# A fused delta-rule attention and two MoE layers: vector work re-queued behind later steps

## The chip, the cores and the metric

The kernel runs on one core of a Trainium2 chip. The metric is the time of one execution in device microseconds (us). Three runs of the kernel before gave 983.3, 986.69 and 988.2 us; their median is 986.69 us. The engines that matter here are TensorE (PE in the profile), VectorE (DVE), ScalarE (ACT), GpSimd (POOL, which here mostly issues DMAs) and SyncE (SP, which only issues DMAs). Each has its own queue of instructions and runs them in the order in which they stand there.

## The reference

Three things are computed one after the other. Shapes are 4 batches, 8 heads, 768 steps of 48 features, so that the attention's output is 3072 tokens of 384 features.

```python
# attention: a delta rule over 768 steps, for each batch and head
k_n = k / (norm(k) + 1e-06)
for t in range(S):
    y[t] = q[t] @ state
    state = state + beta[t] * outer(k_n[t], v[t] - state.T @ k_n[t])
x = y.transpose(0, 2, 1, 3).reshape(3072, 384)
# MoE 1, 384 -> 2048 -> 384
h = maximum(x @ w_in, 0.0); x = (h * h) @ w_out
# MoE 2, 384 -> 768 -> 384
h = maximum(maximum(x @ w1, x @ w2), x @ w3); out = h @ w_out2
```

## The kernel before, in words

The 768 steps are cut into 12 chunks of 64 (`NC`). A chunk of attention is computed in block form: inside a chunk, a triangular system of 64 by 64 per head is inverted in two halves of 32, and the halves are then merged.

**The solve** (`solve32`, `solve`, lines 280 to 288 and 678 to 695) inverts the 32 by 32 halves of two chunks at once on VectorE: a short preparation that begins with a copy of the diagonal (`ss`, L264), then 30 steps of two dependent instructions each (L285 and L287), then one multiplication (L288). The result goes to DRAM (`xt`, `finish32`) and comes back as `xb` and `x1` (`load_x`). There are six solves: chunks 0 and 1 in the prologue, 2 and 3 beside MoE(0) and MoE(1), then 4 and 5, 6 and 7, 8 and 9, 10 and 11 beside MoE(2), (4), (6) and (8). The solve also yields the norms of the keys, which TensorE transposes (`pt`, L277) and ScalarE copies to `normT` (L313).

**The attention of a chunk** (`attention(c)`, lines 383 to 537) is a generator of steps. `st0(p)` multiplies V by the norms (L436, "V's norm" below) and multiplies the keys and queries with the running state (`pA`, `pY`, L447), after which VectorE forms `r` (L450). `zz` transposes `x1` on VectorE (`xT`, L408) and makes `pZ` (L415) from `xb`; `ww` makes `pW` (L424) from `xT` and `z` and ScalarE copies it into `xb` (L431): this is the merge. `mm_u(p)` makes `pU` from `xb` and `r` (L457, copied to `u` at L462), `st2(p)` makes `pY` and the growth of the state `pD` (L497, L475; `Sb` added at L482; `yy` copied at L512), `st3(p)` transposes `yy` (`pT`, L518) and splits it into a high part `xh` (ScalarE, L521) and a low part `xl` (VectorE, L522). p is 0 or 1, two halves of the heads.

**MoE 1 of a chunk** (`moe_a(c)`, lines 540 to 586), called MoE(c) here, has 8 blocks s1 (18 matmuls of `p` from `xh` and `xl`, L552) and 8 blocks s2 (18 matmuls of `px`, L570), s2 two blocks behind s1. Between them ScalarE makes the high part `gh` (L558) and VectorE the low part `gl` (L559), which also frees the PSUM tile of s1 (there are two). The attention of chunk c+1 is interleaved with MoE(c), so that MoE(c+1) can start when `xh` and `xl` of chunk c+1 are there. Beside MoE(0), (1), (3), (5) and (7), `kkps` makes the Gram matrices of later chunks (`pk`, `pq`, L197; stored to DRAM as `kk` and `p`).

**What sets the order.** In the loop over chunks (lines 800 to 834) `steps` advances the main generator MoE(c) by 16 steps and after each one the others at given rates; `later(n, g)` lets n steps pass first and `part(g, n)` takes only n steps of a generator. A scheduler then orders the instructions of each engine by its own estimate of when they are ready. `behind(a, b)` forbids it to put a ahead of b on the same engine; it makes nobody wait for a semaphore. `last_gl[0]` is the newest `gl` and `last_vec[0]` the newest marked VectorE instruction (a transpose `xT` or a low part `xl`).

From MoE(9) on, `w3load` also loads and splits the words of `w1` and `w2`: four VectorE instructions for each piece (L110, L113, L114, L118) and two on ScalarE (L107, L115). Behind MoE(11) the second MoE runs alone (L857, L874).

Of the kernel before, what the change touches and what calls it, by code (L numbers as in the profile page):

```python
# [39 lines left out]
def delta_moe(ctx, tc, kc, ab, kt, vt, beta, beta32, beta16, kq, w_in, w_out, w1, w2, w3, w_out2, out):  # L40
# [32 lines left out]
    parted, last_gl, last_gh = [], [None], [None]  # L73
# [197 lines left out]
    def behind(ins, before):  # L271

        tc.add_manual_dep(ins, before.name, mybir.DependencyInfo(mybir.DependencyClass.NoSync, mybir.DependencyReason.DATA), reason="order")
# [6 lines left out]
    def solve(eng, M, n, u, a, tmp):  # L280

        for j in range(1, n - 1):
            m = n - 1 - j
            tv = tmp[0:u, 0:j * m].rearrange("p (a b) -> p a b", a=j)
            eng.tensor_tensor(out=tv, in0=M[:, 0:j, j].unsqueeze(2).broadcast_to([u, j, m]),  # L285
                              in1=M[:, j, j + 1:n].unsqueeze(1).broadcast_to([u, j, m]), op=ALU.mult)
            yield eng.tensor_tensor(out=M[:, 0:j, j + 1:n], in0=M[:, 0:j, j + 1:n], in1=tv, op=ALU.add)  # L287
        yield eng.tensor_tensor(out=M, in0=M, in1=a.unsqueeze(2).broadcast_to([u, n, n]), op=ALU.mult)  # L288
# [44 lines left out]
    def load_x(c):  # L333

        k21 = att.tile([128, B * Q, 32], F32, name="k21", tag="k21", bufs=1)
        x1 = att.tile([128, U2, 32], F32, name="x1", tag="x1", bufs=1)
        ds = []
        for t in range(2):
            if c:
                ds.append(pool.dma_start(k21[64 * t + 32:64 * t + 64], kk_d[c][32:64, t, :, 0:32]))  # L340
            for h in range(2):
                o, hs = 64 * t + 32 * h, slice(32 * h, 32 * h + 32)
                i = (pool if c else (nc.sync, act)[t]).dma_start(xb[o:o + 32, :, hs], xt_d[c][h, t].rearrange("u j i -> j u i"))
                if c:
                    ds.append(i)
                else:
                    x_loaded.append(i.ins)
        for t in range(2):
            for g in range(2):
                o = 64 * t + 32 * g  # L350
                i = (pool if c else (nc.sync, act)[t]).dma_start(x1[o:o + 32], xt_d[c][0, t, U2 * g:U2 * g + U2].rearrange("u j i -> j u i"))
                ds.append(i)
        for i in x_after:
            if c:
                for d in ds:
                    behind(d.ins, i)
        return k21, x1
# [21 lines left out]
    xh, xl, masked, last_act, last_vec = {}, {}, {}, [None], [None]  # L379
    second_out = []  # L380
    ops, normed, solved, solve_after, x_loaded = [], [], [], [], []

    def attention(c):
# [7 lines left out]
        def fresh(name, p, i, shape):  # L391
            if name == "r" and p and not c:
                t = pkp.tile(shape, F32, name="r1", tag="r1")
            else:
                t = att.tile(shape, F32, name=name, tag=name, bufs=1 if name == "r" else 2)
            tiles[c, p][i] = t
            return t
# [7 lines left out]
        def zz(k21, x1):  # L405
            xT = att.tile([128, U2, 32], F32, name="xT", tag="xT", bufs=1)
            z = k21[:, 0:U2]
            last_vec[0] = vec.transpose(out=xT, in_=x1).ins  # L408
            if c == 1:
                behind(last_vec[0], last_gl[0])  # L410
            pZ = ps_at.tile([128, U2, 32], F32, name="pZ", tag="at")
            for u in spread:
                for t in range(2):
                    lower = k21[last(t), u] if c else kss[u // U2][last(t), 0, u % U2, 0:32]
                    pe.matmul(pZ[part_(t, u), u % U2], lower, xb[last(t), u, 32:64], start=True, stop=True)  # L415
            last_act[0] = act.activation(out=z, in_=pZ, func=AF.Copy, scale=-1.0).ins
            merge.extend((xT, z))
# [15 lines left out]
        def st0(p):  # L433
            kq_, v = tiles[c, p][0:2]
            vn = v if c else fresh("r", p, 6, [128, U2, D])
            i = vec.tensor_mul(out=vn, in0=v, in1=normT[:, c, U2 * p:U2 * p + U2].unsqueeze(2).broadcast_to([128, U2, D]))  # L436
            if c < 2:
                behind(i.ins, last_gl[0] if c else solved[0])
            if not c:
                return  # L440
            pA = ps_at.tile([128, U2, D], F32, name="pA", tag="at")
            pY = ps_y.tile([128, U2, D], F32, name="pY", tag="y")
            tiles[c, p][8] = pY
            for u in range(U2):
                for i, ps in enumerate((pA, pY)):
                    for t in range(2):
                        pe.matmul(ps[half(t ^ i), u], kq_[feat(t), u, i], Sb[feat(t), U2 * p + u],  # L447
                                  start=not i or u == 0, stop=not i, skip_group_check=bool(i))
            r = fresh("r", p, 6, [128, U2, D])
            vec.tensor_sub(out=r, in0=v, in1=pA)  # L450
# [73 lines left out]
        k21, x1 = load_x(c)  # L524
# [1 line left out]
            load_att(c, 0)  # L526
        load_att(c, 1)
        if c:
            order = ((st0, 0),), ((zz, (k21, x1)),), *(((),) if c == 1 else ()), ((ww, 0),), ((mm_u, 0),), ((st2, 0),), ((st0, 1), (st3, 0)), ((mm_u, 1),), ((st2, 1),), ((st3, 1),)
        else:  # L530
            order = ((st0, 0), (st0, 1)), ((zz, (k21, x1)),), ((ww, 0),), ((mm_u, 0), (mm_u, 1)), ((st2, 0), (st2, 1)), ((st3, 0), (st3, 1)), ((state, 0), (state, 1))
        for fs in order:
# [117 lines left out]
    def part(g, n):  # L650
        for _ in range(n):
            next(g, None)
            yield
# [5 lines left out]
    if True:  # L659
# [18 lines left out]
        def solve32(g, load=(nc.sync, nc.sync), store=((nc.sync,) * 2,) * 2, landing=0):  # L678
            M, a, ready, norm = start32(g, load)
            for _ in range(landing):  # L680
                yield
            if landing:
                prep_after[:] = last_gl
            nm = ready()
            if not landing:
                normed.append(norm(nm))
            yield
            for n, i in enumerate(solve(vec, M, 32, 64 * len(HALVED[g]), a, tmp32)):
                for j in solve_after:
                    behind(i.ins, j)  # L690
                ops.append(i.ins)
                if landing and n == 12:
                    norm(nm)
                yield
            finish32(g, M, store)

        def later(n, g):
            for _ in range(n):
                yield
            yield from g  # L700
# [99 lines left out]
        for c in range(NC):  # L800
            extra = []
            if c + 1 < NC:
                extra.append((9 / 15.0, attention(c + 1)) if c > 1 else (13 / 15.0, later(3, attention(1))) if not c else (17 / 15.0, later(8, attention(2))))
            if c == 0:
                ws = weights()
                for _ in range(2):
                    next(ws)
                extra.insert(0, (1.0, ws))
            if c in KK:
                extra.append((1.0, kkps(HALVED[1], (at,), pool)) if c == 0 else (0.8, later(5, kkps(HALVED[2], (at,)))) if c == 1 else (0.6, kkps(HALVED[KK[c]], (at,))))  # L810
            if c in SOLVE:
                solve_next = solve32(SOLVE[c], landing=16 if c == 8 else 10) if c else solve32(1, (pool,) * 2)
                extra.append((5.0, later(45, part(solve_next, 20))) if c == 0 else (6.0 if c == 8 else 4.0, solve_next))
            if c == 1:
                extra.insert(0, (6.0, solve_next))
            if c == 1:
                kc_after.clear()
            if c == 1:
                solve_after[:] = last_vec
                prep_after.clear()  # L820
            if c == 2:
                solve_after.clear()
            if c == 9:
                after[:] = last_gl
                load_w3s = w3load((0, 1))
            if 9 <= c < NC - 1:
                extra.append((0.4, part(load_w3s, 6)))
            if c == NC - 1:
                pr.close()
                wb = ctx.enter_context(tc.tile_pool(name="wb", bufs=1, side="right", reuse_waits="tile"))  # L830
                first = []
                extra.append((0.6, chain(load_w3s, w3load((2,)))))
                extra.append((0.5, later(2, x2_steps(0, wb, first))))
            steps(moe_a(c, gp), *extra)
# [114 lines left out]
```

## Time and profile before

| what | value |
|---|---|
| median of three runs | 986.69 us |
| the profiled execution | 983.45 us |
| its span, first to last instruction | 981.7 us |
| mean granted clock of TensorE over the span | 0.956 of full speed |
| TensorE busy | 902.9 us (92%) |
| VectorE busy | 452.8 us (46%) |
| ScalarE busy | 414.3 us (42%) |
| GpSimd busy | 154.1 us (16%) |

The profiled execution takes 1.75 us more than its span, and is 3.24 us below the median. The page has TensorE busy in nine tenths or more of nearly every fortieth of the span from 147 us on; its waits lie ahead of that and at a few places behind. The views used below are the table by stretches (cut where the first matmul of each MoE(c) starts), the timeline of an engine with the idle time before each instruction, the groups of instructions by line with a mean duration, and the chain that ended last.

### The profile page before, as it was taken

Reading aid. Unit: us, or ns where it says so; the run is one execution under the profiler, and the core shown is the slowest. Engines: PE = TensorE matmul, PEld = TensorE weight load, DVE = VectorE, ACT = ScalarE, POOL = GpSimd, SP = SyncE. Lnnn points to the kernel's source line nnn. Section 1 sums busy time; section 2 is a strip of 40 time slices with the busy share of each in tenths; the row PEclk is TensorE's granted clock in tenths of the full one; section 3 lists DMA queues with packets and bytes.
Section 4 is the critical chain, followed back from the end, with each engine's and each line's share of the span. In section 5 each row is a group of like instructions: output and inputs, shape, how many; then the busy total and the mean of one; then the engine's idle time right before and its main releaser. Section 6 shows DMA issues by size and latency. Waiting matters only on the chain.

```text
span 981.7 us, 26638 instructions
## 1 busy us (share of the span) xinstructions
PE 902.9 (92%) x11674; PEld 830.0 (85%) x11674; DVE 452.8 (46%) x976; ACT 414.3 (42%) x817; POOL 154.1 (16%) x257
## 2 busy tenths in 40 slices
PE   5057879999999999999999899999999999999998
PEld 4057768989899999999999799999888888888887
DVE  2979577129422852394238344446621323232221
ACT  1946873345344544444444356565411212121111
POOL 3133310321312132114111320000100000000000
PEclk8567988989999999999999999999999999999999
DMA  9948721571554155415522532134400100000001
GB/s 206 320 111 254 224 83 50 138 193 54 147 142 128 54 147 154 116 54 147 157 75 65 141 113 85 49 101 135 137 9 25 41 24 25 17 17 17 17 17 41
DMA packets 77413, 98.84 MB, mean 101 GB/s; under 512 B 37312, under 2 KB 55024, under 8 KB 77296
## 3 DMA queue, kind: packets, MB, share of 16 engines
q1 hardware_dynamic: 55232, 54.29, 19.6%
q0 software_dynamic: 12992, 36.35, 12.8%
q10 hardware_dynamic: 9072, 6.49, 2.3%
q8 instruction: 92, 1.51, 0.6%
q14 instruction: 25, 0.20, 0.1%
HBM read 72.45 MB, written 24.64 MB: 99 GB/s over the span
## 4 chain that ended last, share of the span: by engine, by line
PE 69%; DVE 10%; DMA 8%; issue 6%; ACT 4%; POOL 2%; ACTq 0%; SPq 0%; DVEq 0%; POOLq 0%
PE p L857 23%; PE p L552 15%; PE px L570 14%; PE po L874 8%; DVE buf L287 3%; DVE buf L285 3%; PE pU L457 2%; DMA xb<-xt 2%; PE pY L497 2%; DMA v<-in_vt_dram 1%; DMA buf<-kk 1%; DMA xt<-buf 1%; PE pZ L415 1%; PE pk L197 1%; PE pW L424 1%
## 5 line engine op out<-in xcount | busy, mean ns | idle before, releaser
L570 PE MATMUL px<-gh,wout 128*128 128x256 f32 x1152 | 218.8, 289 | 1.2 <-issue 1.2
L857 PE MATMUL p<-x_h,w 128*128 128x512 f32 x648 | 203.5, 395 | 0.0
L570 PEld LDWEIGHTS px<-gh,wout 128*128 128x128 f32 x1152 | 180.9, 193 | 3.8 <-issue 1.1
L552 PE MATMUL p<-xh,win_h 128*128 128x256 f32 x576 | 169.6, 295 | 4.8 <-DVE gl L559 3.4
L552 PE MATMUL p<-xl,win_h 128*128 128x256 f32 x576 | 166.3, 292 | 3.7 <-DVE xl L522 3.7
L552 PE MATMUL p<-xh,win_l 128*128 128x256 f32 x576 | 165.8, 289 | 0.0
L570 PE MATMUL px<-gl,wout 128*128 128x256 f32 x576 | 164.3, 285 | 0.0
L857 PEld LDWEIGHTS p<-x_h,w 128*128 128x128 f32 x648 | 121.7, 188 | 27.0
L559 DVE TENSOR_TENSOR gl<-p,gh 128x512 fp32r<-128x512 f32 x96 | 65.9, 687 | 154.0 <-ACT gh L558 153.6
L857 PE MATMUL p<-x_l,w 128*128 128x512 f32 x324 | 128.1, 395 | 0.0
L552 PEld LDWEIGHTS p<-xh,win_h 128*128 128x128 f32 x576 | 113.0, 196 | 8.3 <-DVE gl L559 4.2
L556 ACT ACTIVATE p<-p 128x512 f32<-128x512 f32 x96 | 56.1, 584 | 149.3 <-PE p L552 145.6
L552 PEld LDWEIGHTS p<-xl,win_h 128*128 128x128 f32 x576 | 112.5, 197 | 4.9 <-DVE xl L522 3.9
L552 PEld LDWEIGHTS p<-xh,win_l 128*128 128x128 f32 x576 | 113.2, 196 | 0.3
L570 PEld LDWEIGHTS px<-gl,wout 128*128 128x128 f32 x576 | 111.1, 193 | 0.3
L863 DVE TENSOR_TENSOR mx<-p,mx 128x512 f32<-128x512 f32 x36 | 24.9, 691 | 128.6 <-PE p L857 128.6
L865 ACT CAST hh<-mx 128x512 fp32r<-128x512 f32 x36 | 22.3, 621 | 127.6 <-DVE mx L864 127.6
L857 PEld LDWEIGHTS p<-x_l,w 128*128 128x128 f32 x324 | 61.0, 188 | 14.5
L287 DVE TENSOR_TENSOR buf<-buf 128x30 f32<-128x30 f32 (+9 forms) x180 | 59.5, 331 | 5.4
L285 DVE TENSOR_TENSOR buf<-buf 128x30 f32<-128x30 f32 (+9 forms) x180 | 59.2, 329 | 5.2
L558 ACT CAST gh<-p 128x512 fp32r<-128x512 f32 x96 | 56.3, 587 | 2.7
L557 ACT ACTIVATE p<-p 128x512 f32<-128x512 f32 x96 | 55.9, 583 | 2.8
(171 smaller groups left out, 1337.2 us busy)
## 6 DMA issues: line engine op xcount, KB each, us to landing
kq<-in_kc_dram POOLq DMA_DIRECT2D x22, 448.0 KB, 4.6
raw<-in_moe_w_dram SPq DMA_DIRECT2D x18, 384.0 KB, 3.1
p<-p POOLq DMA_DIRECT2D x22, 256.0 KB, 3.2
raw<-in_moe_w_out_dram SPq DMA_DIRECT2D x14, 384.0 KB, 3.7
v<-in_vt_dram POOLq DMA_DIRECT2D x24, 192.0 KB, 4.0
ktp<-in_kt_dram POOLq DMA_DIRECT2D x24, 192.0 KB, 3.3
xr<-x SPq DMA_DIRECT2D x12, 384.0 KB, 3.0
out_dram<-os ACTq DMA_DIRECT2D x24, 192.0 KB, 1.9
```

Of the source, the lines that this page charges most:

```text
L285: eng.tensor_tensor(out=tv, in0=M[:, 0:j, j].unsqueeze(2).broadcast_to([u, j, m]), in1=M[:, j, j + 1:n].unsqueeze(1).broadcast_to([u, j, m ...
L287: yield eng.tensor_tensor(out=M[:, 0:j, j + 1:n], in0=M[:, 0:j, j + 1:n], in1=tv, op=ALU.add)
L552: pe.matmul(p1[:, j], w[:, k, f], x[c][:, k], start=n == 0 and j == 0, stop=n == 8, skip_group_check=True)
L556: act.activation(out=p1, in_=p1, func=AF.Relu)
L557: act.activation(out=p1, in_=p1, func=AF.Square)
L558: last_gh[0] = act.copy(gh, p1).ins
L559: last_gl[0] = vec.tensor_sub(out=gl, in0=p1, in1=gh.bitcast(F32)).ins
L570: pe.matmul(acc[m], w, x[:, j], start=f == 0 and i == 0 and m != 1, stop=f == NF - 1 and i == 2, skip_group_check=True)
L857: pe.matmul(p, w[i][:, k, fs], x[:, k], start=n == 0, stop=n == 8)
L863: vec.tensor_max(out=t, in0=ps[1], in1=t)
L865: act.copy(hh[:, f], t2)
L874: pe.matmul(po[:, 0:DM], x[:, f, js], w[:, f], start=i == 0, stop=i == 17)
```

## The change

Six edits, all of them to the order in which work is queued; no instruction is added or taken out.

1. The transposes `xT` of all chunks from 1 on are placed behind the newest `gl`; before, those of chunk 1 alone.
2. V's norm (L436) of chunks from 2 on is placed behind the newest marked VectorE instruction; before, it was free there.
3. Attention(4) and attention(10) get an empty step between `st0(0)` and `zz`, and beside MoE(3) and MoE(9) a rate of 10/15 in place of 9/15.
4. The transposition of the norms of the second solve is issued at its step 12, as in the later solves, and no longer directly after the preparation.
5. Of the second solve 8 steps in place of 20 are issued beside MoE(0); the rest follows beside MoE(1).
6. Beside MoE(9) the six steps of `w3load` come at a rate of 0.8 from the seventh step on, in place of 0.4 from the first.

```diff
             last_vec[0] = vec.transpose(out=xT, in_=x1).ins
-            if c == 1:
+            if c:
                 behind(last_vec[0], last_gl[0])
...
-            if c < 2:
-                behind(i.ins, last_gl[0] if c else solved[0])
+            behind(i.ins, solved[0] if not c else last_gl[0] if c == 1 else last_vec[0])
...
-            order = ((st0, 0),), ((zz, (k21, x1)),), *(((),) if c == 1 else ()), ((ww, 0),), ((mm_u, 0),), ((st2, 0),), ((st0, 1), (st3, 0)), ((mm_u, 1),), ((st2, 1),), ((st3, 1),)
+            order = ((st0, 0),), *(((),) if c in (4, 10) else ()), ((zz, (k21, x1)),), *(((),) if c == 1 else ()), ((ww, 0),), ((mm_u, 0),), ((st2, 0),), ((st0, 1), (st3, 0)), ((mm_u, 1),), ((st2, 1),), ((st3, 1),)
...
-            if not landing:
+            if not g:
                 normed.append(norm(nm))
...
-                if landing and n == 12:
+                if g and n == 12:
                     norm(nm)
...
-                extra.append((9 / 15.0, attention(c + 1)) if c > 1 else (13 / 15.0, later(3, attention(1))) if not c else (17 / 15.0, later(8, attention(2))))
+                extra.append(((10 if c in (3, 9) else 9) / 15.0, attention(c + 1)) if c > 1 else (13 / 15.0, later(3, attention(1))) if not c else (17 / 15.0, later(8, attention(2))))
...
-                extra.append((5.0, later(45, part(solve_next, 20))) if c == 0 else (6.0 if c == 8 else 4.0, solve_next))
+                extra.append((5.0, later(45, part(solve_next, 8))) if c == 0 else (6.0 if c == 8 else 4.0, solve_next))
...
-                extra.append((0.4, part(load_w3s, 6)))
+                extra.append((0.4, part(load_w3s, 6)) if c > 9 else (0.8, later(6, part(load_w3s, 6))))
```

What this does to the queues is seen at three places. In the rows of the changed kernel every line number above 436 is one lower than in the kernel before (L521 there is L522 here). First, VectorE's queue at the end of MoE(0), before the change: `xl` is the low part of the second half of chunk 1, without which MoE(1) cannot go on; L285 and L287 are steps of the second solve.

```order
L482 TENSOR_TENSOR Sb<-pD,Sb 128x384
L287 TENSOR_TENSOR buf<-buf 128x12x19
L285 TENSOR_TENSOR buf<-buf 128x234
L287 TENSOR_TENSOR buf<-buf 128x13x18
L522 TENSOR_TENSOR xl<-pT,xh 128x3x128
L285 TENSOR_TENSOR buf<-buf 128x238
```

The same place in the changed kernel, from the last low parts of w_out's pieces (L135) on:

```order
L135 TENSOR_TENSOR wout_1519<-raw,wout_1519 128x384
L481 TENSOR_TENSOR Sb<-pD,Sb 128x384
L521 TENSOR_TENSOR xl<-pT,xh 128x3x128
L287 TENSOR_TENSOR buf<-buf 128x8x23
L285 TENSOR_TENSOR buf<-buf 128x198
L436 TENSOR_TENSOR v<-v,normT 128x384
L287 TENSOR_TENSOR buf<-buf 128x9x22
```

`xl` stood behind solve step 13 and now stands ahead of the second half of step 8; a norm of V follows it.

Second, TensorE's queue in the last quarter of MoE(1), before the change: `pZ` is the first product of chunk 2's merge, `p_2410` the last s1 of MoE(1), after which two and a half blocks s2 are still to come.

```order
L552 MATMUL p_2410<-xl,win_h 128x256
L552 MATMUL p_2410<-xh,win_h 128x256
L415 MATMUL pZ<-xb,k_2054 32x32 x31
L552 MATMUL p_2410<-xh,win_l 128x256
L552 MATMUL p_2410<-xl,win_h 128x256
```

The same merge in the changed kernel:

```order
L569 MATMUL px<-gh,wout_1519 128x256 x2
L569 MATMUL px<-gl,wout_1519 128x256
L415 MATMUL pZ<-xb,k_2054 32x32 x32
L424 MATMUL pW<-k_2054,xT 32x32 x32
L197 MATMUL pk<-big 64x64 x2
L197 MATMUL pq<-big 64x64 x2
```

The `px` rows there are the last of MoE(1): the whole merge and everything of attention(2) after it now stands behind the last matmul of MoE(1), with only Gram matrices (`pk`, `pq`) and the products of chunk 3's `st0` between its steps.

Third, VectorE's queue at the start of MoE(9), before the change: L408 is the transposition for chunk 10, whose `x1` comes by DMA from the last solve; the rows L558 or L559 are the low parts of MoE(9).

```order
L450 TENSOR_TENSOR r<-v,pA 128x384
L559 TENSOR_TENSOR gl<-p_8141,gh 128x512
L408 STREAM_TRANSPOSE xT<-x_8194 128x256
L559 TENSOR_TENSOR gl<-p_8166,gh 128x512
L559 TENSOR_TENSOR gl<-p_8249,gh 128x512
L436 TENSOR_TENSOR v<-v,normT 128x384
```

And in the changed kernel:

```order
L436 TENSOR_TENSOR v<-v,normT 128x384
L449 TENSOR_TENSOR r<-v,pA 128x384
L558 TENSOR_TENSOR gl<-p_8141,gh 128x512
L558 TENSOR_TENSOR gl<-p_8166,gh 128x512
L558 TENSOR_TENSOR gl<-p_8249,gh 128x512
L558 TENSOR_TENSOR gl<-p_8292,gh 128x512
L408 STREAM_TRANSPOSE xT<-x_8194 128x256
L436 TENSOR_TENSOR v<-v,normT 128x384
```

The transposition moved from behind the first `gl` to behind the fourth, and on TensorE the `pZ` of chunks 4 and 10 stands one block s1 later than before. Chunk 4 in MoE(3) changes in the same way.

## Rows read from the trace of the kernel before

**Rows 1.** Stretches: length, busy us (instructions) of PE, PEld, DVE, ACT, POOL; PEclk; DMA.

```profile
144.27:207.57 63.30, 57.25 (x992) 54.22 (x991) 30.09 (x70) 23.42 (x47) 15.50 (x26) 0.87 0.43 119
207.57:253.72 46.15, 46.09 (x764) 43.97 (x762) 33.20 (x90) 21.76 (x48) 6.98 (x11) 1.00 0.30 85
253.72:306.39 52.67, 51.00 (x999) 48.77 (x999) 12.88 (x23) 23.08 (x47) 15.59 (x26) 0.97 0.62 165
...
351.76:401.63 49.87, 49.78 (x998) 47.44 (x999) 12.97 (x23) 22.99 (x47) 15.57 (x26) 1.00 0.66 174
...
497.15:543.03 45.88, 45.82 (x744) 43.63 (x744) 33.72 (x90) 21.75 (x48) 6.99 (x11) 1.00 0.19 62
543.03:594.48 51.45, 47.92 (x743) 45.03 (x743) 19.23 (x39) 25.78 (x53) 15.59 (x26) 0.97 0.50 135
```

**Rows 2.** Timeline of TensorE, end of MoE(0): start, us, in brackets idle before.

```profile
131.21 0.90 PE L518 MATMUL pT<-ident,yy 128*128 128x128 f32 x3 [2.80 <-ACT normT L313]
...
142.97 0.55 PE L518 MATMUL pT<-ident,yy 128*128 128x128 f32 x3 [1.38 <-ACT yy L512]
149.40 0.58 PE L552 MATMUL p<-xl,win_h 128*128 128x256 f32 x1 [3.72 <-DVE xl L522]
```

**Rows 3.** Timeline of ScalarE, the same stretch.

```profile
124.55 1.29 ACT L512 COPY yy<-pY 64x192 f32<-64x192 f32 x4
...
126.66 1.12 ACT L125 ACTIVATE big<-big 128x384 uint16<-128x384 uint16 x1
...
143.56 0.48 ACT L521 CAST xh<-pT 128x384 fp32r<-128x384 f32 x1 [0.64 <-PE pT L518]
```

**Rows 4.** Timeline of VectorE, 139 to 178 us.

```profile
148.79 0.55 DVE L522 TENSOR_TENSOR xl<-pT,xh 128x384 fp32r<-128x384 f32 x1
...
167.05 1.22 DVE L288 TENSOR_TENSOR buf<-buf,a 128x1024 f32<-128x1024 f32 x1
...
177.60 0.45 DVE L408 STREAM_TRANSPOSE xT<-x 128x256 f32<-128x256 f32 x1 [1.65 <-DMA x<-xt]
```

**Rows 5.** Chain that ended last, in order of time: MoE(1)'s third s1 and later blocks.

```profile
157.51 2.35 PE p L552 x18
...
161.78 2.16 PE p L552 x18
```

**Rows 6.** Groups by line, 179 to 198 us: busy us, mean ns; idle before.

```profile
L431 ACT COPY xb<-pW 32x256 f32<-32x256 f32 x4 | 1.5, 363 | 1.1 <-PE pW L424 1.0
L512 ACT COPY yy<-pY 64x192 f32<-64x192 f32 x4 | 1.2, 312 | 3.3 <-PE pD L475 3.3
...
L462 ACT COPY u<-pU 128x384 f32<-128x384 f32 x1 | 0.5, 480 | 0.6 <-PE pU L457 0.6
...
L457 PE MATMUL pU<-r,xb 64*64 64x48 f32 x32 | 1.1, 220 | 0.5 <-ACT xb L431 0.5
...
L415 PE MATMUL pZ<-xb,k 32*32 32x32 f32 x64 | 1.0, 195 | 0.0
```

**Rows 7.** Timeline of TensorE, 195 to 203 us.

```profile
199.59 1.95 PE L457 MATMUL pU<-r,xb 64*64 64x48 f32 x32 [1.84 <-DVE xl L522]
```

**Rows 8.** Timelines of VectorE and TensorE at the merges of chunks 4 and 10.

```profile
265.34 0.45 DVE L408 STREAM_TRANSPOSE xT<-x 128x256 f32<-128x256 f32 x1 [5.84 <-DMA x<-xt]
...
265.61 0.24 PE L415 MATMUL pZ<-xb,k 32*32 32x32 f32 x2 [1.17 <-DMA xb<-xt]
...
554.94 0.45 DVE L408 STREAM_TRANSPOSE xT<-x 128x256 f32<-128x256 f32 x1 [6.12 <-DMA x<-xt]
...
556.01 0.38 PE L552 MATMUL p<-xh,win_h 128*128 128x256 f32 x1 [2.68 <-DVE gl L559]
557.19 0.24 PE L415 MATMUL pZ<-xb,k 32*32 32x32 f32 x2 [0.56 <-DMA xb<-xt]
```

**Rows 9.** Timelines of VectorE and TensorE in MoE(2): the third solve's preparation and chunk 3's merge.

```profile
220.13 0.19 DVE L264 COPY ss<-buf 128x32 f32<-128x32 f32 x1 [1.25 <-DMA buf<-kk]
...
223.23 0.75 PE L424 MATMUL pW<-k,xT 32*32 32x32 f32 x64
```

## The prediction

> **What bounds the kernel now.** I read the table by stretches first, cut at the first matmul of each MoE(c) [rows 1]. TensorE is busy nearly throughout, so the question is what each stretch lasts above its undisturbed length. Two rows give that length: 45.88 us for MoE(8) without Gram matrices, 49.87 us for MoE(5) with them, both at a granted clock of 1.00. Against these, MoE(3) with 52.67 is 2.8 us too long, MoE(9) with 51.45 (no Gram matrices) 5.6 us, and MoE(1) with 63.30 some 13 us. Their PEclk is 0.97, 0.97 and 0.87: at 0.87, a stretch of 63.3 us gives away 0.13 × 63.3 = 8.2 us where TensorE works at its lower level, 1.2 GHz in place of 2.4; 0.97 gives away 1.6 us each.
>
> Next I looked for the waits themselves, on TensorE's timeline. At the end of MoE(0) it stands 2.80 us for the norms of the second solve, 1.38 us for `yy`, and 3.72 us in MoE(1)'s first block for `xl` [rows 2]. That last one is a queue, not work: ScalarE has `xh` at 143.56 + 0.48 = 144.04 [rows 3], and VectorE makes `xl` only at 148.79 [rows 4], behind solve steps that nobody waits for yet. In MoE(1)'s tail `pU` waits 1.84 us because `xl` stands behind a norm of V [rows 7]. In MoE(3) and MoE(9) the transposition of `x1` holds VectorE idle for 5.84 and 6.12 us until its DMA lands; at MoE(9) a `gl` behind it is late, and TensorE waits 2.68 us for the `gl` and 0.56 us for `xb`; at MoE(3) it waits 1.17 us for `xb` [rows 8].
>
> **The end of MoE(0) (edits 4, 5).** `pT` no longer waits for the norms, but its own input moves back: `yy`, finished at 124.55 + 1.29 = 125.84, now stands behind two more word instructions of about 0.9 to 1.1 us [rows 3], so it ends near 127.6 and TensorE stands some 3.5 us in another place. The 2.80 us are thus mostly exchanged, with the dip of the clock that follows such a gap. I put MoE(1)'s first matmul at 143.5 in place of 144.27 (between 141 and 146). From there on `xl` follows `xh` at once, as it stands ahead of step 8's second half: the 3.72 us and the clock's dip around them go. What is late next on VectorE is the solve: steps 8 to 30 now lie in MoE(1), between the `gl`. Two s1 take 4.3 us [rows 5], chunk 2's `pA` and `pY` 2.2 us [rows 6], some Gram matrices 0.5 us, and the first `gl` comes up to 1 us late behind ten solve steps: the third s1 starts at 143.5 + 7.8 = 151.3, not at 157.51 [rows 5]. **Gain 6.2 us**, bounds 3 and 8.
>
> **MoE(1) and the merge behind it (edits 1, 2, 5).** From its third s1 on MoE(1) has 14 blocks of 2.16 us [rows 5], 30.2 us, and 0.7 us of Gram matrices, so its last matmul is at 182.2. `xb` must have landed by then. Before, the solve ended at 167.05 + 1.22 = 168.27 and `x1`, the last to land, was there at 177.60 [rows 4], 9.3 us later. The steps left over take as long as before and are interrupted by five `gl` in place of four, in a MoE(1) that begins earlier, so that I have them end near 167 again; SP now issues Gram stores ahead of the solve's, which I allow 1 us. 178 is ahead of 182.2, so `pZ` doesn't wait. But now the chain of chunk 2 has no MoE matmuls beside it. Its links are `pZ` 1.0, `z` 0.5, `pW` 0.75 (rows 9 show one of 0.75), `xb` 1.5, `pU` 1.1, `u` 0.5, `pY` with `pD` 1.1, `yy` 1.25, `pY` of the other half 1.1, `pT` 0.5, `xh` 0.5, `xl` 0.55, and again `pU`, `u`, `pY` with `pD`, `yy`, `pT`, `xh`, `xl` with 5.5 together [rows 2 to 4, 6]: 15.9 us. Some 18 hand-overs of 0.05 (pT ends at 143.52, `xh` starts at 143.56 [rows 2, 3]) make 16.8. I add 1 us for unseen waits: MoE(2) starts at 200.0, not at 207.57. So of the 6.2 us nothing is lost and **1.4 us more** come, 7.6 together; before, the same end took 50.1 us from the third s1, now 48.7. Bounds of this part are a loss of 10 (rival 1) and a gain of 3.
>
> **MoE(3) and MoE(9) (edits 1, 2, 3).** `pZ` moves behind one more s1, 2.16 us [rows 5]: more than the 1.17 us that MoE(3) shows. At MoE(9) the `gl` no longer stand behind the transposition, so the fourth s1 starts on time, at 556.01 − 2.68 = 553.3, and `pZ` comes 2.16 us later, near 555.5; `xb`, at 557.19 before, must be 1.7 us earlier. It is, for the two norms of V that lay in the solve leave it (about 0.55 us each, as `xl` of the same shape [rows 4], and their waits), and the words of w1 no longer load beside it (edit 6). I take both stretches back to their undisturbed lengths: **2.8 us** and **5.6 us**. Bounds: 0 and 3.2; 2 and 6. What is late next there is `pW`, which needs `xT` behind the fourth `gl`; its s1 ends ahead of it and `pW` stands after another block, so it is covered.
>
> **The rest.** V's norm now stands behind `xl` or behind `xT`. V itself is loaded a chunk ahead, so nothing waits there; were it late, the `gl` behind it would be late too, at a price like the 2.68 us of MoE(9). The words of w1 in MoE(9) (edit 6) put three pieces ahead of `xl` of chunk 10 in place of two; four instructions of about 0.5 us lie in an idle stretch of VectorE, and I count 0.5 us (bounds 0 and 3). POOL's queue changes by one exchange of two loads, at no cost, since both are a chunk early. SP's queue changes as said.
>
> **Sum.** 6.2 + 1.4 + 2.8 + 5.6 − 0.5 = 15.5 us. The profiled execution takes 983.45 us (span 981.7 and 1.75 around it), so the changed one would take 968.0. The median shown lies 3.24 us higher, at 986.69; on it I predict **971 us**.
>
> **Rival 1, the bare merge runs at half clock.** The chain behind MoE(1) has about 15 us of small matmuls (its links on TensorE, chunk 3's `pA` and `pY`, three groups of Gram matrices), with waits for ScalarE between them. Before, a gap of 1.84 us in this very chain [rows 7] was followed by `pU` at 1.95 us where another took 1.1 [rows 6]. If the clock stays at 1.2 GHz from there on, the matmuls cost up to 10 us more: total gain 5.5, 981 us. Against it: the gaps that I expect are 0.3 to 0.6 us, and the gap of 0.5 us ahead of `pU` [rows 6] left it at full speed. The Trainium skill, "TensorE: Matmul & The Clock Gate", section "A second HAM failure mode: psum-queue depth-cycling", says that frequent short idles between groups of matmuls make the clock swing between its two levels; by that rule the time would be the 981 us of this rival. The row with 0.5 us of idle and a fast `pU` speaks against the rule here. 15 in 100.
>
> **Rival 2, the merges of chunks 4 and 10 stay bound by the DMA.** If `xb` lands a block later than I think (its loads share the queue with those of `x1`), the extra step only moves the wait and both stretches keep theirs, as if edits 1 and 3 did nothing: gain 7.1, 979.6 us. For it: both waits were for that DMA [rows 8]. Against: the part that MoE(9) lost to `gl` goes in any case. 12 in 100.
>
> **Rival 3, slower.** In MoE(2), (4), (6) and (8) the transposition for the odd chunk now stands behind L264, the start of the next solve, which waits for Gram matrices from DRAM. In MoE(2) it waited 1.25 us, to 220.13, and `pW`, which needs `xT`, ran at 223.23 [rows 9]. The margin is 3.1 us less the transposition and the hand-over, about 2.5. Each us beyond holds TensorE, with a dip of the clock on top. From 6 us of delay in each of the four it decides: 4 × (3.5 + 1.6) = 20.4 us (1.6 for each dip, as in rows 1) are more than the gain, and 991 us result. Against it: the chain that feeds L264 moves with MoE(2)'s start. 11 in 100, with other losses that I can't name.
>
> **How the numbers follow.** The forecast has 62 in 100; alone it spans 964 to 978 by its terms' bounds. The range takes in rivals 1 and 2 and about half of rival 3: 962 to 985. Changes under 0.5% (4.9 us) can't be told from none in such a measurement. Faster by more holds for the forecast but its slowest cases and for most of rivals 1 and 2: 0.75. Within 0.5%: 0.14. Slower: 0.11.
>
> **What would show it.** Right: no wait of TensorE for `xl` at MoE(1)'s start; MoE(2) starting near 200; after `pZ` of chunk 2 only short waits and a granted clock of 1.00; MoE(3) near 50, MoE(9) near 46; `gl` not behind `xT`. Wrong: PEclk under 0.9 in the 18 us ahead of MoE(2); `pZ` waiting for `xb` in MoE(1), (3) or (9); `pW` waiting for `xT` in an even MoE; VectorE idle at a norm of V with a late `gl` behind it.

## The result and the profile after

The changed kernel takes 978.88 us (median of 12 runs, 972.82 to 983.67) beside 986.17 us of the kernel before (12 runs, 983.25 to 990.94): a ratio of 0.9913, 95% interval 0.9895 to 0.993. That is 7.3 us, about half of the 15.5 that the sum had. The profiled execution takes 980.28 us with a span of 978.6.

The stretches of the changed kernel, with the columns of [rows 1]: MoE(0) to MoE(5), then MoE(7) to MoE(9).

```profile
72.74:145.27 72.53, 58.58 (x1035) 54.45 (x1031) 51.65 (x123) 55.69 (x106) 20.70 (x34) 0.91 0.63 189
145.27:204.87 59.60, 53.40 (x1008) 50.80 (x1001) 29.33 (x69) 24.23 (x52) 15.51 (x26) 0.94 0.51 134
204.87:254.06 49.19, 49.14 (x762) 46.82 (x761) 32.98 (x89) 21.66 (x48) 6.98 (x11) 0.93 0.27 76
254.06:304.79 50.73, 50.67 (x998) 47.93 (x999) 12.53 (x22) 22.63 (x47) 15.59 (x26) 1.00 0.63 167
...
350.16:399.50 49.34, 49.28 (x999) 47.22 (x999) 12.43 (x22) 23.09 (x47) 15.57 (x26) 1.00 0.68 176
444.86:495.51 50.65, 49.71 (x998) 47.40 (x999) 12.44 (x22) 23.01 (x47) 15.57 (x26) 1.00 0.62 153
495.51:541.39 45.88, 45.82 (x743) 43.63 (x744) 33.98 (x91) 21.78 (x48) 6.99 (x11) 1.00 0.21 62
541.39:591.30 49.91, 48.12 (x743) 45.62 (x743) 18.72 (x38) 25.44 (x53) 15.62 (x26) 0.97 0.49 131
```

MoE(0) starts at 72.74, and 1.44 us sooner in the kernel before (71.30), although their code is the same up to there: executions differ by that much, so I compare lengths, not clock times. Against [rows 1] MoE(1) is 3.7 us shorter, MoE(2) 3.0 longer, MoE(3) 1.9 and MoE(9) 1.5 shorter. The gain of MoE(1) is nearly lost again in MoE(2), where PEclk is 0.93.

The timeline of TensorE shows why: the wait of `pY` at the end of MoE(0) first, then the merge of chunk 2 behind MoE(1), in brackets the idle time before.

```profile
129.01 1.49 PE L446 MATMUL pY<-Sb,kq 48*64 48x48 f32 x32 [3.70 <-ACT yy L511]
...
182.97 0.75 PE L415 MATMUL pZ<-xb,k 32*32 32x32 f32 x64
184.28 0.75 PE L424 MATMUL pW<-k,xT 32*32 32x32 f32 x64 [0.56 <-ACT k L416]
186.62 1.14 PE L456 MATMUL pU<-r,xb 64*64 64x48 f32 x32 [0.49 <-ACT xb L431]
188.33 0.26 PE L496 MATMUL pY<-u,p 64*64 64x48 f32 x2 [0.58 <-ACT u L461]
...
195.36 0.32 PE L496 MATMUL pY<-u,p 64*64 64x48 f32 x4 [0.60 <-ACT u L461]
199.79 0.34 PE L496 MATMUL pY<-u,p 64*64 64x48 f32 x1 [3.52 <-issue]
```

The merge is bare, its links wait 0.5 to 0.6 us each as forecast. But in the middle of a `pY` whose first matmuls have run, TensorE is idle for 3.52 us, and the releaser is "issue": nothing that the profile shows was waited for. Such an idle time is called a stand below. The clock follows. Table by windows of the same execution:

```profile
192.00:196.00 4.00, 3.40 (x139) 2.97 (x141) 1.25 (x2) 1.54 (x3) 1.49 (x3) 1.00 1.08 235
196.00:200.00 4.00, 0.47 (x26) 0.35 (x22) 0.00 (x0) 0.00 (x0) 1.65 (x3) 0.73 1.02 219
200.00:204.00 4.00, 4.00 (x104) 3.55 (x102) 1.47 (x3) 2.32 (x6) 1.12 (x2) 0.50 0.95 299
204.00:208.00 4.00, 4.00 (x37) 3.60 (x34) 0.81 (x2) 0.00 (x0) 0.00 (x0) 0.50 0.85 251
208.00:212.00 4.00, 4.00 (x23) 4.00 (x22) 0.00 (x0) 1.73 (x3) 0.00 (x0) 0.56 0.43 72
```

VectorE and ScalarE are empty from 196 to 200 as well, the DMA engines are full (DMA share 1.0), and TensorE then works at 1.2 GHz (0.50) until 211.5.

In MoE(9) no `gl` is late any more, but `pZ` of chunk 10 still waits for the DMA of `xb`; two rows of TensorE's timeline answer to [rows 8]:

```profile
554.66 0.24 PE L415 MATMUL pZ<-xb,k 32*32 32x32 f32 x2 [0.94 <-DMA xb<-xt]
555.42 0.73 PE L415 MATMUL pZ<-xb,k 32*32 32x32 f32 x62 [0.52 <-DMA xb<-xt]
```

### The profile page after: what moved, and what is told of

Same layout as the page of the kernel before. It is cut to its first block, busy times and chain, and to the rows that moved or that the text cites. A ratio compares the mean times of both kernels' runs of the same rounds, so it can differ in the third digit from the quotient of the medians.

```text
span 978.6 us, 26655 instructions
## 1 busy us (share of the span) xinstructions
PE 901.9 (92%) x11674; PEld 828.7 (85%) x11674; DVE 451.4 (46%) x976; ACT 413.8 (42%) x817; POOL 154.4 (16%) x257
## 3 DMA queue, kind: packets, MB, share of 16 engines
q8 instruction: 92, 1.51, 0.7%
## 4 chain that ended last, share of the span: by engine, by line
PE 76%; DVE 11%; ACT 5%; DMA 4%; issue 2%; POOL 1%; ACTq 0%; SPq 0%; DVEq 0%; POOLq 0%
PE p L856 23%; PE p L551 18%; PE px L569 17%; PE po L873 8%; DVE buf L287 3%; DVE buf L285 3%; PE pU L456 2%; PE pY L496 2%; DMA xb<-xt 1%; PE pk L197 1%; PE pY L446 1%; PE pZ L415 1%; PE pA L446 1%; DVE gl L558 1%; PE pW L424 1%
## 5 line engine op out<-in xcount | busy, mean ns | idle before, releaser
L856 PE MATMUL p<-x_h,w 128*128 128x512 f32 x648 | 203.4, 395 | 0.0
L558 DVE TENSOR_TENSOR gl<-p,gh 128x512 fp32r<-128x512 f32 x96 | 66.3, 690 | 188.3 <-ACT gh L557 188.3
L285 DVE TENSOR_TENSOR buf<-buf 128x30 f32<-128x30 f32 (+9 forms) x180 | 59.5, 330 | 5.8
L287 DVE TENSOR_TENSOR buf<-buf 128x30 f32<-128x30 f32 (+9 forms) x180 | 59.5, 330 | 5.2
```

The lines of the kernel that those rows point to most:

```text
L558: last_gl[0] = vec.tensor_sub(out=gl, in0=p1, in1=gh.bitcast(F32)).ins
L856: pe.matmul(p, w[i][:, k, fs], x[:, k], start=n == 0, stop=n == 8)
```

## The experiments

Theory: TensorE's instructions themselves come by DMA. The page of the profile has a queue q8 of kind "instruction" with 92 packets and 1.51 MB, 16 KB each; 11,674 matmuls and as many weight loads make 254 in a packet, if all of these packets are TensorE's. Small matmuls use up such a block in a few us, and where the DMA engines are full the next one is late. Rivals: the small matmuls lower the clock by themselves; or the stand has to do with edits 1 and 2. Ratios are against runs of the kernel before that were taken beside each group of kernels (their medians lie between 986.17 and 987.7 us), so medians of different groups compare only roughly.

| kernel | median us | ratio, 95% interval |
|---|---|---|
| e1_steps: edits 4, 5 | 987.31 | 0.9997, 0.9976 to 1.0019 |
| e2_rest: edits 1, 2, 3, 6 | 978.29 | 0.99, 0.9869 to 0.9931 |
| e7_vec12: edits 1, 2 | 978.09 | 0.9913, 0.9883 to 0.9943 |
| e8_step3: edit 3 | 985.42 | 0.9986, 0.9968 to 1.0005 |
| v_part12: all, 12 solve steps | 978.93 | 0.9912, 0.9887 to 0.9937 |
| e3_nostore: all, Gram stores left out | 973.58 | 0.9871, 0.9843 to 0.9899 |
| e5_reload: all, read-back later | 977.42 | 0.9911, 0.9881 to 0.994 |
| e6_rest_reload: e2, read-back later | 975.43 | 0.9891, 0.9865 to 0.9918 |
| g4_double: e6, extra reads | 978.12 | 0.9898, 0.9868 to 0.9929 |
| g1_two: e6, chunk 10 later | 975.8 | 0.9877, 0.9853 to 0.9901 |
| g2_part14: e5, 14 solve steps | 977.11 | 0.9896, 0.9868 to 0.9924 |
| g3_part14_two: g2, chunk 10 later | 975.89 | 0.9877, 0.9849 to 0.9904 |

### Which edits carry the gain

**e1_steps**, the kernel before with

```diff
-            if not landing:
+            if not g:
-                if landing and n == 12:
+                if g and n == 12:
-... part(solve_next, 20)
+... part(solve_next, 8)
```

> The kernel before with edits 4 and 5 alone. TensorE's order through MoE(0), MoE(1) and the merge of chunk 2 is that of the changed kernel. Theory (TensorE runs out of instructions in the bare merge because the blocks of its program, 16 KB each, come late behind the stores of Gram matrices): it stands some 3.5 us near 196 us in the middle of pY and pD with no releaser, then works at half clock for 13 to 14 us, and of the 7.6 us forecast for these edits 1 to 3 are left: 983 to 985 us beside 986 of before. Rival (the stand in the changed kernel comes from edits 1 and 2): no such gap here, 978 to 980 us.

There was no stand by "issue", so this expectation failed; the time came out at no gain at all. That doesn't make edits 1 and 2 the cause of the stand, as the rival had it: the packet of q8 that starts at 197.2 in the changed kernel starts at 197.8 here, as late, but TensorE was still held by another wait. In place of the stand `pU` of chunk 2 waited for `xl`, as in [rows 7], only longer, and MoE(2) took 48.76 us. The row of TensorE:

```profile
198.59 1.62 PE L457 MATMUL pU<-r,xb 64*64 64x48 f32 x26 [3.66 <-DVE xl L522]
```

And VectorE's timeline of the same execution just ahead of it:

```profile
197.51 0.56 DVE L436 TENSOR_TENSOR v<-v,normT 128x384 f32<-128x384 f32 x1 [5.43 <-DMA v<-in_vt_dram]
197.99 0.55 DVE L522 TENSOR_TENSOR xl<-pT,xh 128x384 fp32r<-128x384 f32 x1
```

V's norm of chunk 3 holds VectorE for 5.43 us, because V itself is still on its way from DRAM, and `xl` stands behind it.

**e2_rest** is the change without those lines.

> The kernel before with edits 1, 2, 3 and 6 alone. By the stretches of the changed kernel's trace these edits give 1.9 us in MoE(3), 0.5 in MoE(5), 1.5 in MoE(9) and cost 0.5 in MoE(7): 3.4 us, so 982 to 983 us beside 986. By the prediction's terms (2.8 + 5.6 - 0.5 = 7.9) it would be 978. MoE(9) should last near 49.9 us and pZ of chunk 10 still wait for xb.

978.29 us, all of the change's gain and more than the stretches had promised (982 to 983). MoE(9) lasts 50.36 us as expected. In the merge TensorE stands by "issue" twice, 0.83 and 1.71 us.

**e7_vec12** keeps the first two edits alone (the transposition behind `gl`, V's norm behind the newest marked instruction).

> The kernel before with edits 1 and 2 alone. In MoE(1)'s end pU no longer waits for xl (1.84 us in before, 3.66 with edits 4 and 5 alone); in MoE(9) no gl stands behind xT (2.68 and 4.09 us), but pZ, which nothing moved, waits for xb for 2 to 3 us there and 1 to 2 us in MoE(3). If the late gl and xl were what counted: 979 to 981 us. If these waits only turn into waits for xb: 983 to 985.

978.09 us, near the first expectation: these two edits carry all that can be measured. In MoE(9) `pZ` now waits 3.16 us for `xb` in this execution; no `gl` is late. MoE(1) and MoE(2) together take 103.51 us, against 109.45 of [rows 1] and 109.81 of e1_steps.

**e8_step3** keeps the third alone (`((),) if c in (4, 10)` and the rate of 10/15).

> The kernel before with edit 3 alone. By MoE(3)'s stretches 1.9 us come from here; in MoE(9) gl still stands behind xT, so that it gives nothing or little there: 984 to 985 us beside 986.5. If the empty step is what frees MoE(9) (xb lands while the other s1 runs): 980 to 982.

985.42 us; the interval holds no change. TensorE's row in MoE(9), the same wait as in [rows 8]:

```profile
558.45 0.58 PE L552 MATMUL p<-xh,win_h 128*128 128x256 f32 x1 [4.12 <-DVE gl L559]
```

MoE(3) shrank by 1.94 us, MoE(9) did not (53.47). In VectorE's queue V's norm waited 5.48 us at 200.98 ahead of `xl`.

### What TensorE waits for in the bare merge

**e3_nostore** leaves out the stores of the Gram matrices of chunks 4 and 5, which then use those of chunks 2 and 3:

```diff
-            kk_store(c, p, ks[:, 0], dma)
+            if cs is not HALVED[2]:
+                kk_store(c, p, ks[:, 0], dma)
-            for t in range(2):
+            for t in range(2 if cs is not HALVED[2] else 0):
+    kk_d[4:6], p_d[4:6] = kk_d[2:4], p_d[2:4]
```

> The changed kernel without the stores of the Gram matrices of chunks 4 and 5 (1 MB in small packets between 166 and 206 us); these chunks read those of chunks 2 and 3, so the output isn't the reference's. TensorE's order and number of instructions stay. Theory (the blocks of instructions come late because the DMA queues are full): the gap of 3.5 us near 196 us shrinks under 1.5 us, the clock stays at 1.00, MoE(2) starts 4 to 6 us sooner and lasts 46.2 us: 970 to 973 us beside 979 of the changed kernel. Rival (TensorE uses up its blocks faster than they can come, whatever else the DMA does): the gap stays at 3 to 4 us and the time at 978 to 979. Second rival (the small matmuls lower the clock by themselves): the gap goes, but the half clock stays, 975 to 976.

The stand of 3.52 us is gone; one of 1.15 is left, at another instruction, and the clock stays up. A row of the timeline and three of the windows:

```profile
202.52 0.25 PE L447 MATMUL pA<-Sb,kq 48*64 48x48 f32 x1 [1.15 <-issue]
```

```profile
192.00:196.00 4.00, 3.52 (x127) 3.03 (x123) 1.25 (x2) 1.40 (x3) 1.20 (x3) 1.00 0.83 244
196.00:200.00 4.00, 3.39 (x151) 3.00 (x153) 1.25 (x2) 2.42 (x7) 3.59 (x6) 1.00 0.96 223
200.00:204.00 4.00, 2.85 (x40) 2.48 (x35) 1.02 (x2) 0.04 (x1) 0.00 (x0) 1.00 0.83 213
```

The same matmuls at the same short waits run at 2.4 GHz throughout in this execution, so the rival that they lower the clock falls. 973.58 us, just above the 970 to 973 expected; some of the gain is MoE(9), which took 46.98 us here. But this kernel moved something else too: the read-back of the Gram matrices of chunk 4 for the solve (L304) no longer has to follow its stores, and went out at 171.7 us in place of 191.3. In the changed kernel that read-back lies in the stand; the DMA view of 194 to 197 us:

```profile
DMA packets 1409, 0.56 MB, mean 185 GB/s; under 512 B 1311, under 2 KB 1311, under 8 KB 1409
## 3 DMA queue, kind: packets, MB, share of 16 engines
q0 software_dynamic: 113, 0.39, 66.9%
q1 hardware_dynamic: 1296, 0.16, 40.3%
```

1311 of 1409 packets are under 512 bytes, but the 113 larger ones of q0 took the greater share of the DMA engines' time (66.9% and 40.3%). q8 has none. From 190 to 194 and from 197 to 199 it has one each; the second starts at 197.2 and ends at 198.4, and TensorE goes on 1.4 us behind it.

**v_part12** asks whether a merge with MoE work in it suffers less (`part(solve_next, 12)`).

> The changed kernel with 12 steps of the second solve beside MoE(0) in place of 8. In the order pZ of chunk 2 then stands 17 px matmuls behind the last s1 of MoE(1), with 31 px matmuls between pZ and pU and five behind pU, so most links of the merge up to pU have MoE work beside them and TensorE uses its instructions more slowly. Theory: the block of instructions is there in time or nearly so, no gap over 1.5 us, MoE(2) starts 3 to 6 us sooner: 971 to 975 us beside 979. Rival (the four more steps in MoE(0) delay its last words and xl, or pZ waits for xb, which the merge then meets sooner): 978 to 981 us.

978.93 us, the rival's number, but not for its reason: the stands remain, ahead of the same instructions as in the changed kernel and in e2_rest.

```profile
201.50 0.20 PE L496 MATMUL pY<-u,p 64*64 64x48 f32 x1 [2.63 <-issue]
208.60 0.23 PE L446 MATMUL pA<-Sb,kq 48*64 48x48 f32 x1 [1.14 <-issue]
```

Counted in matmuls from the program's start, the stands of e2_rest, e5_reload, v_part12 and of the changed kernel come ahead of number 2508, and a second one of the first three, and one each of e3_nostore, g1_two and g4_double, ahead of number 2635: 127 matmuls, 254 instructions, one packet later. In g2_part14 both come one matmul later (2509 and 2636), in g3_part14_two the first alone. The kernel before has such a stand too, in MoE(0), ahead of number 1109, eleven packets earlier but for two matmuls; nine of the thirteen other executions have it there:

```profile
106.03 0.39 PE L570 MATMUL px<-gh,wout 128*128 128x256 f32 x2 [1.24 <-issue]
```

From 60 us on the fourteen executions have 24 stands of 0.5 us and more. Every one of them ends 1.3 to 1.9 us behind the end of a q8 packet. A stand that keeps to a count of instructions and to these packets, in kernels whose order and data differ, speaks for the supply of instructions. What makes a packet late is less clear. In 23 of the 24 the DMA share, taken from 1 us ahead of the stand to its end, was 0.88 to 1.15, but packets under 512 bytes were more than a fifth of all in two alone, the changed kernel's and v_part12's first; and one stand of 0.56 us (e7_vec12, at 474 us) came with the DMA engines idle.

**e5_reload** moves only the read-back, behind the last Gram store:

```diff
+                last_p[0] = dma.dma_start(p_d[c] ...).ins
+                if g == 2:
+                    behind(loaded[0], last_p[0])
```

> The changed kernel with one more order: on SP the read-back of chunk 4's Gram matrices for the solve (L304, 2048 packets of 128 bytes, issued at 191.33 us) stands behind the last store of chunk 5's, so behind the bare merge. TensorE's order stays. Theory, narrowed (these small packets delay the block of instructions): the stand of 2.6 to 3.5 us in the second pY goes or stays under 1 us, the clock stays at 1.00, 972 to 975 us beside 979. Rival (the stores and the loads of keys and queries delay it, as all of them were still there): the gap stays over 2 us, 978 to 979. Second rival (the solve beside MoE(2) starts late for want of the read-back): MoE(2) or MoE(3) longer by 1 us or more, which eats the gain.

The stand shrinks to 1.64 us, between the two expectations, and the clock stays at 1.00 through MoE(1) and MoE(2). Timeline, then stretches:

```profile
200.58 0.25 PE L500 MATMUL pY<-u,p 64*64 64x48 f32 x1 [1.64 <-issue]
...
206.32 0.25 PE L450 MATMUL pA<-Sb,kq 48*64 48x48 f32 x1 [1.43 <-issue]
```

```profile
147.90:203.97 56.07, 51.22 (x1007) 48.79 (x1001) 28.67 (x68) 24.20 (x52) 15.51 (x26) 1.00 0.46 128
203.97:251.90 47.93, 46.44 (x764) 44.15 (x762) 33.61 (x91) 21.64 (x48) 6.98 (x11) 1.00 0.36 95
```

MoE(1) and MoE(2) take 104.0 us together in place of 108.8. The median, 977.42, is not separated from the changed kernel's. With the read-back moved in the same way, the stands of g2_part14 and g3_part14_two at this place are 0.78 and 1.32 us, beside 3.52 and 2.63 us in the changed kernel and v_part12, where it wasn't moved; second stands of 1.43 and 1.38 us remain in e5_reload and g2_part14.

**e6_rest_reload** is the same edit on e2_rest.

> Edits 1, 2, 3 and 6 without 4 and 5, with the same later read-back. Theory: the two stands without a releaser (0.83 us near 199 and 1.71 us near 205 in the kernel with these four edits) go or halve, MoE(2) lasts 46 to 48 in place of 49.55 us, and the time is 974 to 977 us beside 978.3. Rival: no change of either, 978.

No stand by "issue" is left in the merge, MoE(2) lasts 46.64 in place of 49.55 us, and the time is 975.43. **g4_double** puts other small packets back where the read-back had been:

```diff
+        for c in (2, 3) if g == 2 else ():
+            for s in range(2):
+                o = 64 * (c - 2) + 32 * s
+                i = dmas[0].dma_start(M[o:o + 32], units(kk_d[c][..., 32 * s:32 * s + 32], 32 * s, 32))
+                behind(i.ins, stores[-5])
```

> Edits 1, 2, 3 and 6 with the later read-back, and at the place where the read-back stood before, four extra DMAs of the same shape (128-byte packets, twice those of chunk 4's read-back) that read the Gram matrices of chunks 2 and 3 into the solve's tile, where the true read-back overwrites them. Theory (small packets on the DMA rings hold up the blocks of instructions): the block around 198 us comes later, stands without a releaser of 2 to 5 us in the merge with half clock behind them, 979 to 984 us beside 975.4. Rival (the read-back had nothing to do with it, and the difference of 978.3 and 975.4 lies elsewhere): 975 to 976.5.

A stand of 1.14 us is back (less than the 2 to 5 expected), the clock falls behind it, and MoE(2) takes 48.98 us:

```profile
208.21 0.25 PE L456 MATMUL pA<-Sb,kq 48*64 48x48 f32 x1 [1.14 <-issue]
```

```profile
206.15:255.13 48.98, 47.79 (x764) 45.54 (x762) 33.63 (x91) 21.67 (x48) 6.98 (x11) 0.97 0.40 101
```

The median, 978.12, lies between the two expectations; it is 2.7 us above that of e6_rest_reload, which the intervals don't separate. Nor do the traces settle it. Through MoE(2) g1_two has the code of e6_rest_reload, without the extra reads, and its MoE(2) is nearly as long as that of g4_double, behind a stand of 0.59 us:

```profile
206.73 0.25 PE L450 MATMUL pA<-Sb,kq 48*64 48x48 f32 x1 [0.59 <-issue]
```

```profile
205.22:253.71 48.49, 47.85 (x764) 45.55 (x762) 33.68 (x91) 21.66 (x48) 6.98 (x11) 0.96 0.39 101
```

And e7_vec12, which through MoE(2) has the code of e2_rest with the read-back at its old place (issued at 192.7), shows no stand in the merge:

```profile
204.72:251.67 46.95, 46.37 (x763) 44.05 (x762) 33.56 (x91) 21.79 (x48) 7.00 (x11) 1.00 0.38 98
```

So single executions of the same code differ by as much as the read-back was to explain. That stands come from late instructions is well supported; that the read-back, or small packets, make them late is not shown.

### Towards a faster version

**g1_two** gives chunk 10 a second empty step (`((),) * (1 + c // 10)`, rate 11/15) on e6_rest_reload, **g2_part14** puts `part(solve_next, 14)` on e5_reload, **g3_part14_two** does both.

> Edits 1, 2, 3 and 6 with the later read-back (975.4 us), and for chunk 10 a second empty step ahead of zz with a rate of 11/15: in the order its pZ stands 18 px matmuls (2.2 us) later. Theory (pZ of chunk 10 still waits for xb's DMA, by an amount that differs from run to run): no wait of pZ in MoE(9), which lasts 45.9 to 46.5 us in place of 48.0, 973.5 to 975 us. Rival (the later merge delays chunk 10 as a whole, xh and xl come late): MoE(9) 48 us or more, 975.5 to 977.

> The changed kernel (all six edits) with the later read-back and 14 steps of the second solve beside MoE(0), whose merge of chunk 2 has 23 px matmuls between pZ and pW. Theory (edits 4 and 5 are worth nothing only because the merge is then bare and its instructions late): against edits 1, 2, 3 and 6 with the same read-back (975.4) the gain at MoE(1)'s start now stays: 971 to 974 us. Rival (edits 4 and 5 only move the wait at the end of MoE(0) from pT to pY and lengthen the solve in MoE(1), worth nothing in any merge): 975 to 978.

> The last two together. If both do what their theories say: 970 to 972.5 us; if neither: 975 to 978.

With the second empty step no `pZ` waits in MoE(9), which lasts 46.19 us (46.18 in the third kernel), as its theory has it; yet the median is that of e6_rest_reload (by the ratios it is 0.9877 beside 0.9891, also not separated). 14 solve steps gave 977.11, inside the rival's range: the medians show no gain of edits 4 and 5 in either merge. Whether they are worth nothing stays open, because in the profiled executions MoE(3) starts 177.1 to 178.3 us behind MoE(0) in e5_reload, g2_part14 and g3_part14_two, and 179.2 and 180.5 in e6_rest_reload and g1_two. All three stay at 975 to 977 us. The best versions (e6_rest_reload, g1_two, g3_part14_two) are some 3 us below the changed kernel by their medians; their intervals overlap with its.

## Why the prediction was right and wrong

The direction was right. The sum of 15.5 was twice too large, and its largest term stood at the wrong edits. That the time still lies in the stated range is in part luck: a gain of edits 1 and 2 that no term of the sum held stood in for the one lost at edits 4 and 5.

**MoE(1)'s start (6.2 us, edits 4 and 5).** What happens there was right. `xl` no longer waits, `pY` waits 3.70 us in its place (forecast 3.5), and MoE(1) starts at 145.27 - 1.44 = 143.83 (143.5); its third s1 at 151.98 - 1.44 = 150.5 (151.3). The third s1 starts 79.3 to 82.1 us behind MoE(0) in the seven executions with these edits (with 8 to 14 solve steps beside MoE(0)) and 84.4 to 86.9 in the seven without, so this gain is no accident of one profile. The step that failed is "of the 6.2 us nothing is lost": alone these edits give 0.9997, and with the other four the time is 978.88 us, and 978.29 without them. The end of MoE(1) is set by chunk 2's chain, from the end of the solve through `xb` to `xl`, and that doesn't begin sooner because MoE(1) does. In e2_rest the solve ends 4 us sooner than with all six edits; VectorE's row L288 of the two executions, which started within 0.1 us of each other (MoE(0) at 72.64 and 72.74):

```profile
163.66 1.23 DVE L288 TENSOR_TENSOR buf<-buf,a 128x1024 f32<-128x1024 f32 x1
```

```profile
167.62 1.23 DVE L288 TENSOR_TENSOR buf<-buf,a 128x1024 f32<-128x1024 f32 x1
```

Twelve solve steps fewer beside MoE(0) come back as a later end of the solve and a later merge: chunk 2's first `pZ` is at 179.00 in e2_rest, with MoE(1)'s blocks still to run beside it, and at 182.97 with all six edits. The time that TensorE won is spent in the bare merge.

**V's norm (edit 2, without a term of its own).** "V itself is loaded a chunk ahead, so nothing waits there" is the step that hid the largest gain. The prediction saw that `xl` stood behind a norm of V, but not that the norm itself waited for its DMA; VectorE's timeline of before, in MoE(1):

```profile
162.21 0.56 DVE L436 TENSOR_TENSOR v<-v,normT 128x384 f32<-128x384 f32 x1 [2.27 <-DMA v<-in_vt_dram]
...
198.50 0.56 DVE L436 TENSOR_TENSOR v<-v,normT 128x384 f32<-128x384 f32 x1 [4.42 <-DMA v<-in_vt_dram]
198.98 0.55 DVE L522 TENSOR_TENSOR xl<-pT,xh 128x384 fp32r<-128x384 f32 x1
```

The first holds the solve, the second is behind the 1.84 us of [rows 7] and the half clock after it. With edits 1 and 2 both norms run without a wait, and e7_vec12 alone has the whole gain. The two were not tried apart. One part is edit 2's: the solve, which ends ahead of the transpositions that edit 1 moves, ends 92.3 to 95.0 us behind MoE(0)'s start in the five executions with these edits and without 4 and 5, and 97.0 and 97.8 us in before and e8_step3. How the rest divides isn't shown.

**The merge behind MoE(1) (1.4 us).** The last `px` ends at 183.04 - 1.44 = 181.6 (182.2 forecast), the short waits are 0.4 to 0.6, `pZ` waits for nothing. Not foreseen was the stand of 3.52 us for instructions and the half clock behind it; MoE(2) starts at 203.4 on before's time, not at 200.0, and is 3.0 us longer.

**MoE(3) and MoE(9).** 1.9 in place of 2.8 us: in this order MoE(3)'s undisturbed length is 50.7, found in every kernel with edit 3, so it was the yardstick, MoE(5), that was off. In MoE(9) 1.5 of 5.6: "it is [1.7 us earlier]" failed. `xb` was late again: the wait behind the one extra step was 0.6 to 1.9 us in seven of the eight executions that also have edit 1, and there was none in the two with the second empty step. The single profile of before also understated what was to be had: MoE(9) took 53.01 us in e1_steps, which is the same there, and 53.47 in e8_step3, not 51.45. That is one reason why medians moved more than stretches.

**The rest.** The words of w1 cost nothing that shows (MoE(10) 45.73 both times). Rival 1 came about by its result, not by its mechanism: half clock in the merge, but behind the stand. Five waits of 0.44 to 0.60 us between groups of small matmuls left the clock at 1.00; it fell to 0.50 only in the stand of 3.52 us. The Trainium skill, "TensorE: Matmul & The Clock Gate", section "A second HAM failure mode: psum-queue depth-cycling", tells of a kernel in which frequent short idles between groups of matmuls made the clock swing between its two levels; the five waits of this trace did not. Rival 2 was half right (chunk 10), rival 3 wrong: MoE(4), (6) and (8) keep 45.37, 45.37 and 45.88 us, and TensorE has no wait in MoE(2).

Open: the profile of e7_vec12 (983.8 us) lies 5.7 us above its median. Its MoE(0) took 76.23 us, the longest of the fourteen executions, and its MoE(9) 52.51; why MoE(0) varies from 72.5 to 76.2 us isn't known. Nor is it known how often the late instructions occur in executions without a profile.

## What to carry to other kernels

An instruction that an order places in front of others has to be looked up in the trace with its own waits: V's norm waited for a DMA, and everything behind it on VectorE waited along. Time won at the start of a stage is lost where the stage's end hangs on a chain that was not shortened; follow that chain, not TensorE's work. And a stretch of small matmuls needs its instructions delivered: look for idle time without a releaser there, and try it with less DMA traffic beside it. Which traffic matters, these runs leave open.

## What the runs showed of the hardware

TensorE can run out of instructions; this is concluded from the following and not recorded as such. It shows as an idle time with the releaser "issue", at the same count of instructions in different kernels (ahead of matmul 2508 and 2635, 254 instructions apart), and it ended 1.3 to 1.9 us behind the end of a 16 KB packet of the queue of kind "instruction" in all 24 cases of 0.5 us and more. The longest took 3.52 us. The DMA share was 0.88 to 1.15 in 23 of them.

The clock did not follow the length of a stand alone: 3.52 us in the changed kernel and 0.59 us in g1_two were followed by 13.7 and 3.4 us at 1.2 GHz, while stands of 1.64 and 1.43 us in e5_reload left it at 2.4 GHz.
